# Weight parts made anew or kept in SBUF, a later turn in the attention, and the decode of the second layer's weights spread over three engines

## The chip, the cores and the metric

The kernel runs on one core of a Trainium2 chip. The metric is the device time of one execution in microseconds (us), the median of three timed runs. Engines are called by the names of the profile: PE (TensorE, the matmuls), PEld (its weight loads), DVE (VectorE), ACT (ScalarE), POOL (GpSimd) and SP (the queue that issues most DMAs).

## The reference, cut to what matters

```python
# attention: batch 4, heads 8, sequence 576, head size 64
q_s = softmax(q, axis=-1); k_s = softmax(k, axis=sequence)
kv  = einsum('bhsd,bhse->bhde', k_s, v)
x   = einsum('bhsd,bhde->bhse', q_s, kv)           # as 2304 tokens x 512
# first layer: 4 experts of width 1024, every token through all of them
out = sum_e p[:, e] * (relu(x @ w1[e]) @ w2[e])
# second layer, width 2048; its two weights come as 64-bit floats
h = out @ w_in; g = h * sigmoid(1.702 * h); result = g @ w_out
```

## The kernel before, in words

All matmuls are made of split numbers: an operand is cut into a high part and the rest (names ending in `h`/`l` or `_hi`/`_lo`), and a product is three matmuls, high by high, high by low and low by high. The high part is a cast on ACT, the low part a subtraction on POOL or DVE.

**Units.** A layer is cut into units of 256 hidden columns: 16 in the first layer (4 experts by 4), 8 in the second. The tokens are cut into groups 0 (1024 tokens), 1 (512) and 2 (768). Each layer makes two passes over its units, one for group 0 and one for groups 1 and 2 together. One visit of a unit is an *inst* (51 of them, numbers 0 to 50 are the suffixes in the names `a11_7`, `w20_6`), and inst and group make a *step*. The first three units are done before group 0 is whole, for its left half L (insts 0 to 2) and then its right half R (insts 3 to 5).

**Weight parts.** From a unit's weights, loaded as `ra` (first matrix) and `rc` (second), come the parts `a11, a12, a22, s1` to `s4` (or `a11, a12, a21, a22` for insts 0 to 5) in ten buffers of pool `w1p`, and `w20, w21` in four buffers of `w2p`. On the first visit they are made (`hi_w1`, `lo_w1`, `hi_w2`, `lo_w2`) and stored to DRAM (`store_part`: `k_a<-a`, `k_s<-s`, `k_w<-w`); on later visits they are loaded from there (`new_part`: `a<-k_a`, `w<-k_w`). `again` says which.

**Order.** The order of the work is written out by hand: up to step 5 the string `START` names every operation in turn; from step 6 on `step()` runs five stages (`STAGES`), each of them a few matmul products (`m1` to `m7`), evictions (`p1c`, `u2c`, `u3c` on ACT, `u2a`, `u3a`, `p1a` on DVE), the activation of the step before (`rc lc` and so on: `h_hi` on ACT, `h_lo` on DVE) and, in the stages `TILES` and `REST`, the second product `mm2` of the step before: per tile of 128 tokens six matmuls `po`, then `acc` on DVE (on ACT the first time). At the end of a stage `prepare` makes parts of the next inst, and `pump` advances a background generator: the attention of batches 2 and 3 (`attention`, one list of turns per head pair, a new pair every 8 stages), later the decode of the 64-bit weights (`decode`, 32 tiles of 128x512, 1.25 yields per stage). Each engine runs its instructions in the order written, so one that waits holds up everything behind it on its engine.

**The lines that matter:** L491 the product `pb` of the attention (needs `dg`, L487 on DVE); L506 the product `pk`; L110 a helper for copies; L646 the stores of attention output (`x_moe<-xo`); L656 to L659 `to_x2`, which transposes the first layer's output (`pt`), copies it (`xt`) and stores it (`x_ffn<-xt`, through two buffers `xo`); L803 to L824 the decode: masks of the upper word (`ds`, `dt`), and the lower word times the exponent plus the rest (`do`); L885 and L889 `h_lo`; L952 `po`; L964 and L973 `acc`.

```python
turns = ["km", "qm qs", "", "", "kg kgm", "qe", "", "ks ksv", "qu qn", "ke", "", "", "pk", "", "bd"]
"moe": ("-m5 -u3c m1 p1c -u3a", "m2 p1a REST", "-m6 -rc -rb -m7 -lc -u2a",
        "m3 u2c m4 -lb -rd ra -ld la", "TILES"),
```

Of the kernel before, what the change touches and what calls it, by code (L numbers as in the profile page):

```python
# [22 lines left out]
def tile_linear_attention_moe_gelu(  # L23
# [609 lines left out]
    def put_x(j, t0, w, src, eng, first):  # L633

        d, o = t0, None
        while d < t0 + w:
# [12 lines left out]
    def to_x2(i, ti, lt):
# [417 lines left out]
    def step(k_, tiles, before):  # L1067
# [65 lines left out]
        oa22:1 rz:1_2 rr:1_2 bd0:1_2 bd1:1_2@A qu:1_0 qs:1_1@G oa12:1 ha12:2 kg:1_1 qe:1_2 y0:s1 rz:1_0 kgm:1_1 rr:1_0
        q:1_3 ha22:2 bd0:1_0 qu:1_2 la12:2@G bd1:1_0@A qe:1_1 pk:1_3 ow20:0 la22:2@G z0:s1 qu:1_1 qp:1_2 qp:1_0 qr:1_2
        rc:6 qr:1_0 qn:1_2@G rz:1_3 qm:1_3 a1:s2 rr:1_3 bd0:1_3 c1:s2 bd1:1_3@A kdg:1_1 qp:1_1 oa12:0 qs:1_3@V t1:1_2
        qT1:1_2@A qr:1_1 ow21:0 qe:1_3 ks:1_1 a2:s2 ksv:1_1 qn:1_1@G ra:s2 px1:1_2 la:s2 ke:1_1 oa22:2 xf1:1_2@V
        t0:1_2 pk:1_1 qu:1_3 oa11:2 qT0:1_2@V ow20:1 wh0:2 t0:1_1 qp:1_3 qn:1_0@V px0:1_2 wh1:2 qT0:1_1@A qr:1_3
        wl1:2@G rz:1_1 xf0:1_2@A rr:1_1 c2:s2 bd1:1_1@V rc:s2 oa21:0 bd0:1_1 lc:s2 t1:1_0 qn:1_3@G t0:1_0 qT1:1_0@A
        px0:1_1 oa12:2 qT0:1_0@A px1:1_0 xf0:1_1@V px0:1_0 xf1:1_0@A wl0:2@V t0:1_3 xf0:1_0@V qT0:1_3@A ha11:3 t1:1_3
        t1:1_1 qT1:1_3@V px0:1_3 ha21:3 qT1:1_1@V px1:1_3 xf0:1_3@V ha12:3 px1:1_1 xf1:1_3@A y2:s1 xf1:1_1@V ow21:2  # L1140
        open Hb12:b0 y3:s1 z2:s1 Lb12:b0@V ha22:3 y0:s2 ow20:2 z3:s1 Hb22:b0 y1:s2 z0:s2 Lb22:b0@V wh0:3 wh1:3 ha11:4
        y2:s2 z1:s2 y3:s2 z2:s2 ha21:4 z3:s2 a1:s3 c1:s3 St1:b0@V Ht1:b0 ha12:4 ha22:4 a2:s3 Lt1:b0@G c2:s3 ra:s3
# [134 lines left out]
```

## Time and profile before

| | us |
|---|---|
| median of three timed runs (1230.03 to 1230.43) | 1230.19 |
| the profiled execution, its own time | 1235.11 |
| its span, first to last instruction | 1233.3 |
| PE busy | 1209.0 (98%) |
| DVE busy | 850.4 (69%) |
| ACT busy | 464.7 (38%) |
| POOL busy | 358.7 (29%) |

The chain of work that ended last lies on PE for 86% of the span and on DVE for 9%. The mean DMA rate is 183 GB/s. The granted TensorE clock is full in all but one of the 40 slices of the page. In the trace an entry in square brackets is the engine's idle time in front of an instruction and what ended it.

### The profile page before, as it was taken

What the parts mean: (1) busy time and instruction counts of PE and PEld (TensorE: products, weight loads), DVE (VectorE), ACT (ScalarE), POOL (GpSimd) and SP (SyncE); (2) the same over time, 40 slices, a digit from 0 to 9 for tenths busy, and PEclk for the clock granted to TensorE, in tenths of its full rate; (3) what the DMA queues carried; (4) which work ended last, traced back from release to release, by engine and by line L of the source; (5) the groups of instructions that cost most, each with busy time, mean ns of one, the idle gap of its engine ahead of it and who ended that gap; (6) DMA issues with size and microseconds to landing.
All of it is one profiled execution on the core that took longest, in us unless ns stands there. A gap on an engine that the chain in (4) does not pass through costs nothing.

```text
span 1233.3 us, 17497 instructions
## 1 busy us (share of the span) xinstructions
PE 1209.0 (98%) x6276; PEld 1043.9 (85%) x6276; DVE 850.4 (69%) x1416; ACT 464.7 (38%) x1010; POOL 358.7 (29%) x389
## 2 busy tenths in 40 slices
PE   8999899999999999999999999999999999999998
PEld 7878688887888899899899889898788889899997
DVE  7875778767567759998999975577355774454554
ACT  5544345433434352222122222145645544333332
POOL 4424657554553001111112331025454500000000
PEclk9999899999999999999999999999999999999999
DMA  8884966664566366666566632535655655334323
GB/s 199 250 303 141 324 210 203 204 230 149 198 217 226 105 198 213 212 209 211 194 194 221 202 110 69 196 121 186 232 203 213 228 170 161 111 107 122 108 92 86
DMA packets 134423, 225.86 MB, mean 183 GB/s; under 512 B 30400, under 2 KB 62144, under 8 KB 133696
## 3 DMA queue, kind: packets, MB, share of 16 engines
q1 hardware_dynamic: 124832, 220.02, 55.2%
q10 hardware_dynamic: 9504, 4.72, 1.3%
q8 instruction: 50, 0.82, 0.3%
q14 instruction: 37, 0.30, 0.1%
HBM read 137.40 MB, written 87.29 MB: 182 GB/s over the span
## 4 chain that ended last, share of the span: by engine, by line
PE 86%; DVE 9%; DMA 4%; ACT 1%; issue 1%; SPq 0%; POOL 0%; ACTq 0%; DVEq 0%
PE po L952 43%; PE px L836 21%; PE pz L836 10%; PE py L836 5%; DVE acc L964 2%; DVE h_lo L885 2%; DMA w64o<-in_moe_w_out 1%; PE pk L506 1%; PE p L378 1%; DMA x_ffn<-xt 1%; PE ca_R L836 1%; PE cc_R L836 1%; DMA q<-in_q 1%; DVE dso L803 1%; PE px L531 1%
## 5 line engine op out<-in xcount | busy, mean ns | idle before, releaser
L952 PE MATMUL po<-w,h_hi 128*128 128x512 f32 x1728 | 538.4, 393 | 2.4 <-DVE xt L110 2.0
L952 PEld LDWEIGHTS po<-w,h_hi 128*128 128x128 f32 x1728 | 320.8, 189 | 65.2 <-DVE xt L110 2.9
L952 PE MATMUL po<-w,h_lo 128*128 128x512 f32 x864 | 337.7, 391 | 3.2 <-DVE h_lo L885 3.2
L964 DVE SCALAR_TENSOR_TENSOR acc<-po,pr,acc 128x512 f32<-128x512 f32 x270 | 194.6, 745 | 70.1 <-PE po L952 69.7
L952 PEld LDWEIGHTS po<-w,h_lo 128*128 128x128 f32 x864 | 162.8, 188 | 39.4 <-DVE h_lo L885 4.5
L110 ACT COPY u<-px 128x384 f32<-128x384 f32 (+2 forms) x138 | 65.3, 473 | 237.7 <-PE px L836 230.3
L973 DVE TENSOR_TENSOR acc<-po,acc 128x512 f32<-128x512 f32 x126 | 85.7, 689 | 58.5 <-PE po L952 57.4
L866 DVE TENSOR_TENSOR u<-pz,u 128x384 f32<-128x384 f32 (+2 forms) x138 | 75.4, 546 | 52.9 <-ACT u L110 52.1
L774 POOL TENSOR_TENSOR s<-s,s 128x256 fp32r<-128x256 f32 x94 | 80.1, 860 | 74.2 <-ACT s L768 59.7
L787 POOL TENSOR_TENSOR w<-rc,w 128x512 fp32r<-128x512 f32 x46 | 60.4, 1314 | 86.6 <-ACT w L781 71.2
L774 POOL TENSOR_TENSOR a<-ra,a 128x256 fp32r<-128x256 f32 x69 | 53.4, 774 | 90.0 <-ACT a L768 80.0
L879 ACT ACTIVATE h_hi<-px 128x256 fp32r<-128x256 f32 (+2 forms) x45 | 21.8, 484 | 144.3 <-PE px L836 144.2
L885 DVE SCALAR_TENSOR_TENSOR h_lo<-u,h_hi 128x256 fp32r<-128x256 f32 (+2 forms) x90 | 63.7, 732 | 12.5 <-ACT h_hi L879 12.3
L823 POOL TENSOR_TENSOR doi<-doi,dti 128x512 f32<-128x512 f32 x16 | 21.0, 1312 | 161.1 <-DVE doi L820 155.0
L762 POOL TENSOR_TENSOR s<-ra 128x256 f32<-128x256 f32 x48 | 40.5, 844 | 75.8 <-DMA ra<-wi 49.8
L866 DVE TENSOR_TENSOR p<-py,p 128x384 f32<-128x384 f32 (+2 forms) x69 | 37.8, 548 | 33.6 <-PE py L836 30.1
L781 ACT CAST w<-rc 128x512 fp32r<-128x512 f32 x48 | 29.6, 620 | 72.2 <-PE po L952 71.5
L879 ACT ACTIVATE h_hi<-u 128x256 fp32r<-128x256 f32 (+2 forms) x90 | 46.3, 515 | 16.0 <-DVE u L866 16.0
L823 POOL TENSOR_TENSOR doo<-doo,dto 128x512 f32<-128x512 f32 x16 | 21.3, 1330 | 103.7 <-DVE doo L820 91.6
L110 ACT COPY p<-px 128x384 f32<-128x384 f32 (+2 forms) x69 | 32.9, 477 | 37.7 <-PE px L836 37.5
L768 ACT CAST s<-s 128x256 fp32r<-128x256 f32 x96 | 36.8, 404 | 24.0 <-POOL s L762 17.1
L889 DVE TENSOR_TENSOR h_lo<-sc,h_hi 128x512 fp32r<-128x512 f32 (+2 forms) x24 | 13.4, 559 | 44.3 <-ACT h_hi L881 44.3
(312 smaller groups left out, 2470.2 us busy)
## 6 DMA issues: line engine op xcount, KB each, us to landing
w<-k_w SPq DMA_DIRECT2D x54, 512.0 KB, 4.5
k_w<-w SPq DMA_DIRECT2D x48, 512.0 KB, 5.1
a<-k_a SPq DMA_DIRECT2D x84, 256.0 KB, 2.8
k_s<-s SPq DMA_DIRECT2D x84, 256.0 KB, 5.2
s<-k_s SPq DMA_DIRECT2D x84, 256.0 KB, 3.3
k_a<-a SPq DMA_DIRECT2D x75, 256.0 KB, 5.2
ra<-in_moe_w SPq DMA_DIRECT2D x19, 512.0 KB, 4.3
rc<-in_moe_w SPq DMA_DIRECT2D x16, 512.0 KB, 6.1
```

The source lines that it names most:

```text
L110: (eng.copy if eng is A else eng.tensor_copy)(o, i)
L762: G.tensor_tensor(out=o, in0=block_w(m, l), in1=block_w(m, r), op=op)
L774: eng.tensor_tensor(out=lo, in0=block_w(m, x), in1=hi.bitcast(F32), op=ALU.subtract)
L787: eng.tensor_tensor(out=lo, in0=raw[m, 1][:, c, :], in1=hi.bitcast(F32), op=ALU.subtract)
L823: G.tensor_tensor(out=o, in0=o, in1=t.bitcast(F32), op=ALU.add)
L836: T.matmul(ps, a[:, kk, :], b[:, kk, :], start=(start and n == 0), stop=(stop and n == 5), skip_group_check=True,)
L866: return lambda _: V.tensor_tensor(out=y[o], in0=y[ps], in1=y[o], op=ALU.add)
L879: A.activation(hi, y[c], AF.Relu)
L885: V.scalar_tensor_tensor(out=lo, in0=y[c], scalar=0.0, in1=hi.bitcast(F32), op0=ALU.max, op1=ALU.subtract)
L952: T.matmul(ps, a, b, start=(n == 0), stop=(n == 3 * FT - 1))
L964: V.scalar_tensor_tensor(out=acc[ti], in0=ps, scalar=pe, in1=acc[ti], op0=ALU.mult, op1=ALU.add)
L973: V.tensor_tensor(out=acc[ti], in0=ps, in1=acc[ti], op=ALU.add)
```

## The change

It has eight edits.

1. Insts 3 and 4 (the right half of units 1 and 2) use the parts of insts 1 and 2, which stay in SBUF (`HOME`); the right half visits the units in the order 1, 2, 0, so that only inst 5 loads parts back.
2. `w20` and `w21` are no longer stored and loaded back, but made anew at each visit (`again` is true for them in inst 5 alone). `rc` is loaded for each visit.
3. They are made at the end of stages 2 and 3 of an inst's first step, not 1 and 3.
4. In the attention of batches 2 and 3, `ks ksv` and all later turns come one stage later.
5. Its stores `x_moe<-xo` are issued by ACT, not by SP.
6. `xt` is always copied by ACT (before: by DVE in the second layer's steps), and the first `acc` of the second layer by DVE (before: ACT).
7. The decode of a tile takes 5 instructions on DVE (before 7), 2 on ACT (0) and 2 on POOL (1).
8. A filler of 432 instead of 56 words at the right end of SBUF.

```diff
-        turns = [... "kg kgm", "qe", "", "ks ksv", ...]
+        turns = [... "kg kgm", "qe", "", "", "ks ksv", ...]
-            copy(V if stage[1] else A, o, pt.rearrange("p k t -> p (k t)"))
+            copy(A, o, pt.rearrange("p k t -> p (k t)"))
-    turns = [(g, "L") for g in range(AHEAD)] + [(g, "R") for g in range(AHEAD)]
+    turns = [(g, "L") for g in range(AHEAD)] + [(g, "R") for g in (*range(1, AHEAD), 0)]
+    HOME = {AHEAD + n: 1 + n for n in range(AHEAD - 1)}
...
-        names = (PLAIN if m < NPLAIN else STRASSEN) + ("w20", "w21")
+        if m in HOME:
+            continue
+        names = PLAIN if m < NPLAIN else STRASSEN
         again.update({(m, x): (u, x) in had for x in names})
+        again.update({(m, x): m == NPLAIN - 1 for x in ("w20", "w21")})
...
+        V.tensor_scalar(
+            out=t, in0=top, scalar1=3, scalar2=0x007FFFF8, op0=ALU.logical_shift_left, op1=ALU.bitwise_and
+        )
         yield
-        V.tensor_scalar(
-            out=s, in0=s, scalar1=float(896 << 20), scalar2=8.0, op0=ALU.subtract, op1=ALU.mult
-        )
+        A.activation(o, low, AF.Copy, scale=2.0**-52)
+        A.activation(s, s, AF.Copy, bias=-float(896 << 23), scale=8.0)
+        yield
         V.scalar_tensor_tensor(
             out=s, in0=top, scalar=-(1 << 31), in1=s, op0=ALU.bitwise_and, op1=ALU.bitwise_or
         )
-        yield
-        V.tensor_scalar(
-            out=t, in0=top, scalar1=3, scalar2=0x007FFFF8, op0=ALU.logical_shift_left, op1=ALU.bitwise_and
-        )
         V.tensor_tensor(out=t, in0=t, in1=s, op=ALU.bitwise_or)
         yield
-        V.scalar_tensor_tensor(
-            out=o, in0=low, scalar=2.0**-52, in1=s.bitcast(F32), op0=ALU.mult, op1=ALU.mult
-        )
+        G.tensor_tensor(out=o, in0=o, in1=s.bitcast(F32), op=ALU.mult)
         G.tensor_tensor(out=o, in0=o, in1=t.bitcast(F32), op=ALU.add)
...
-                if s in (1, 3) and (m, s // 2) not in W2:
+                if s in (2, 3) and (m, s - 2) not in W2:
```

What this does to the order of the instructions, at three places. On PE, in step 7, after the product `pz4` and ahead of the four tiles `po3_0` to `po3_3` of step 6 (batch 2, head pair 0 of the attention). Before:

```order
L836 MATMUL pz4_0_1644<-t1lA_1191,s1_7_1489 128x512
L836 MATMUL pz4_0_1644<-t1hA_1190,s1_7_1489 128x512
L491 MATMUL pb_2_0_0_1670<-dg2_0_0_1633,ones_88 96x128
L952 MATMUL po3_0_1673<-w20_6_1439,h_hi_91 128x512 x2
L952 MATMUL po3_0_1673<-w20_6_1439,h_lo_92 128x512
```

With the change:

```order
L837 MATMUL pz4_0_1603<-t1lA_1167,s1_7_1452 128x512
L837 MATMUL pz4_0_1603<-t1hA_1166,s1_7_1452 128x512
L953 MATMUL po3_0_1628<-w20_6_1428,h_hi_91 128x512 x2
...
L953 MATMUL po3_3_1652<-w20_6_1428,h_lo_92 128x512
L953 MATMUL po3_3_1652<-w21_6_1458,h_hi_91 128x512 x2
L953 MATMUL po3_3_1652<-w21_6_1458,h_lo_92 128x512
L491 MATMUL pb_2_0_0_1683<-dg2_0_0_1592,ones_88 96x128
```

The product `pb`, which needs `dg` from DVE, stands behind the four tiles instead of ahead of them.

On DVE, in the decode, around tile o2 (`dso2`, `dto2`, `doo2`) and the `h_lo<-px` of inst 22 that the tiles wait for. Before:

```order
L803 TENSOR_SCALAR dso2_6212<-w64o2_6190 128x512
L804 TENSOR_SCALAR dso2_6212<-dso2_6212 128x512
L866 TENSOR_TENSOR p123_1_6209<-py23_1_6217,p123_1_6209 128x256
L964 SCALAR_TENSOR_TENSOR acc16_10_4620<-po22_10_6225,pr_89,acc16_10_4620 128x512
L964 SCALAR_TENSOR_TENSOR acc16_11_4629<-po22_11_6233,pr_89,acc16_11_4629 128x512
L808 TENSOR_SCALAR dso2_6212<-dso2_6212 128x512
L811 SCALAR_TENSOR_TENSOR dso2_6212<-w64o2_6190,dso2_6212 128x512
L815 TENSOR_SCALAR dto2_6213<-w64o2_6190 128x512
L818 TENSOR_TENSOR dto2_6213<-dto2_6213,dso2_6212 128x512
L885 SCALAR_TENSOR_TENSOR h_lo_92<-px22_2_6071,h_hi_91 128x384
```

With the change:

```order
L807 TENSOR_SCALAR dso2_6174<-w64o2_6150 128x512
L808 TENSOR_SCALAR dso2_6174<-dso2_6174 128x512
L811 TENSOR_SCALAR dto2_6175<-w64o2_6150 128x512
L867 TENSOR_TENSOR p123_1_6169<-py23_1_6180,p123_1_6169 128x256
L967 SCALAR_TENSOR_TENSOR acc16_10_4540<-po22_10_6188,pr_89,acc16_10_4540 128x512
L967 SCALAR_TENSOR_TENSOR acc16_11_4549<-po22_11_6196,pr_89,acc16_11_4549 128x512
L818 SCALAR_TENSOR_TENSOR dso2_6174<-w64o2_6150,dso2_6174 128x512
L821 TENSOR_TENSOR dto2_6175<-dto2_6175,dso2_6174 128x512
L886 SCALAR_TENSOR_TENSOR h_lo_92<-px22_2_6030,h_hi_91 128x384
```

The subtraction and multiplication on `dso2` has gone from DVE, and ahead of this `h_lo` two instructions of the tile stand where four stood. The two new copies on ACT stand between `p123_1` and `h_hi<-px22_2`.

On SP, in the second layer, inst 36 (`rc37` is the load for inst 37). Before:

```order
L745 DMA rc37_8740<-wo32_106 128x2x512
L713 DMA k_w21_35_8663<-w21_35_8660 128x1024
L713 DMA k_s3_36_8691<-s3_36_8688 128x512
L713 DMA k_a22_36_8695<-a22_36_8692 128x512
L713 DMA k_s4_36_8699<-s4_36_8696 128x512
L713 DMA k_a11_37_8737<-a11_37_8734 128x512
L713 DMA k_w20_36_8785<-w20_36_8782 128x1024
L713 DMA k_a12_37_8818<-a12_37_8815 128x512
```

With the change:

```order
L749 DMA rc37_8745<-wo32_106 128x2x512
L717 DMA k_s3_36_8697<-s3_36_8694 128x512
L717 DMA k_a22_36_8701<-a22_36_8698 128x512
L717 DMA k_s4_36_8705<-s4_36_8702 128x512
L717 DMA k_a11_37_8742<-a11_37_8739 128x512
L717 DMA k_a12_37_8818<-a12_37_8815 128x512
```

Two stores of 512 KB are gone from each visit in a first pass.

## Rows read from the trace of the kernel before

**Rows 1.** Line 1 of the page: busy time, share of the span, instructions.

```profile
PE 1209.0 (98%) x6276; PEld 1043.9 (85%) x6276; DVE 850.4 (69%) x1416; ACT 464.7 (38%) x1010; POOL 358.7 (29%) x389
```

**Rows 2.** Stretches: from:to, length, busy us (count) per engine, clock, DMA share, GB/s.

```profile
446.00:715.00 269.00, 264.65 (x1463) 238.69 (x1462) 249.32 (x457) 64.70 (x155) 49.87 (x41) 1.00 0.63 204
...
100.00:150.00 50.00, 45.32 (x186) 36.15 (x185) 33.67 (x42) 20.87 (x45) 32.52 (x36) 0.93 0.81 251
250.00:300.00 50.00, 48.31 (x231) 39.28 (x230) 36.49 (x54) 19.54 (x42) 25.32 (x29) 0.97 0.59 207
```

**Rows 3.** Timeline of PE, 126 to 140 us: start, us, instruction, idle before.

```profile
136.29 0.74 PE L491 MATMUL pb<-dg,ones 128*96 128x128 f32 x2 [4.68 <-DVE dg L487]
136.68 1.20 PE L952 MATMUL po<-w,h_hi 128*128 128x512 f32 x2
...
139.38 1.05 PE L952 MATMUL po<-w,h_hi 128*128 128x512 f32 x2
```

**Rows 4.** Timelines of DVE, ACT and SP ahead of that wait.

```profile
132.81 0.69 DVE L885 SCALAR_TENSOR_TENSOR h_lo<-px,h_hi 128x512 fp32r<-128x512 f32 x1 [2.26 <-ACT h_hi L879]
134.30 1.93 DVE L487 TENSOR_SCALAR dg<-ident,gm 128x128 f32<-128x128 f32 x1
...
131.36 0.40 ACT L768 CAST a<-ra 128x256 fp32r<-128x256 f32 x1 [5.28 <-issue]
...
123.16 0.72 SPq L713 DMA_DIRECT2D k_w<-w  x1
...
124.77 1.00 SPq L741 DMA_DIRECT2D ra<-in_moe_w  x1
```

**Rows 5.** Timelines of DVE, POOL and PE, 283 to 300 us.

```profile
285.81 7.04 DVE L885 SCALAR_TENSOR_TENSOR h_lo<-u,h_hi 128x512 fp32r<-128x512 f32 x1 [0.27 <-ACT h_hi L879]
...
285.07 1.79 POOL L466 TENSOR_TENSOR qn<-q,qu 96x768 f32<-96x768 f32 x1 [0.55 <-DVE qu L462]
...
294.17 1.61 PE L506 MATMUL pk<-v,ke 96*128 96x129 f32 x12 [1.69 <-DVE acc L964]
```

**Rows 6.** Timeline of PE in the decode: the three waits, and a tile's start.

```profile
606.21 0.51 PE L952 MATMUL po<-w,h_lo 128*128 128x512 f32 x1 [1.55 <-DVE h_lo L885]
606.55 0.63 PE L952 MATMUL po<-w,h_hi 128*128 128x512 f32 x2
...
607.92 0.62 PE L952 MATMUL po<-w,h_hi 128*128 128x512 f32 x2
...
708.05 0.44 PE L836 MATMUL pz<-b22hmoe,s 128*128 128x384 f32 x1 [1.19 <-DVE u L866]
...
713.58 0.50 PE L952 MATMUL po<-w,h_lo 128*128 128x512 f32 x1 [1.60 <-DVE h_lo L885]
```

**Rows 7.** Timeline of DVE, 596 to 612 us: the `h_lo` of inst 22.

```profile
605.60 0.55 DVE L885 SCALAR_TENSOR_TENSOR h_lo<-px,h_hi 128x384 fp32r<-128x384 f32 x1
```

**Rows 8.** Groups by line and shape: count, busy us, mean ns, idle before.

```profile
L964 DVE SCALAR_TENSOR_TENSOR acc<-po,pr,acc 128x512 f32<-128x512 f32 x270 | 194.6, 745 | 70.1 <-PE po L952 69.7
L787 POOL TENSOR_TENSOR w<-rc,w 128x512 fp32r<-128x512 f32 x46 | 60.4, 1314 | 86.6 <-ACT w L781 71.2 <-PE po L952 15.3
L781 ACT CAST w<-rc 128x512 fp32r<-128x512 f32 x48 | 29.6, 620 | 72.2 <-PE po L952 71.5 <-DMA rc<-in_moe_w 0.7
L823 POOL TENSOR_TENSOR doo<-doo,dto 128x512 f32<-128x512 f32 x16 | 21.3, 1330 | 103.7 <-DVE doo L820 91.6 <-issue 7.2 <-PE px L836 4.9
L820 DVE SCALAR_TENSOR_TENSOR doo<-w64o,dso 128x512 f32<-128x512 uint32 x16 | 10.9, 682 | 0.0
L808 DVE TENSOR_SCALAR dso<-dso 128x512 int32<-128x512 int32 x16 | 7.6, 477 | 0.1
```

**Rows 9.** Timelines of PE and DVE, 862 to 882 us; then landings of `x_ffn<-xt`.

```profile
873.70 0.72 PE L952 MATMUL po<-w,h_hi 128*128 128x512 f32 x2 [1.97 <-DVE xt L110]
...
869.33 0.69 DVE L110 COPY xt<-pt 128x512 f32<-128x512 f32 x1 [3.72 <-DMA x_ffn<-xt]
...
DMA to landing us min/median/max: 2.6/3.9/8.6
```

More of the change, by code (lines that the diff above doesn't have):

```diff
@@ L542, in attend2 @@
             group(g)
-        turns = ["km", "qm qs", "", "", "kg kgm", "qe", "", "ks ksv", "qu qn", "ke", "", "", "pk", "", "bd"]
+        turns = ["km", "qm qs", "", "", "kg kgm", "qe", "", "", "ks ksv", "qu qn", "ke", "", "", "pk", "", "bd"]
         turns += [f"t{g} qT{g}" for g in range(NG_)] + [""] + [f"px{g} xf{g}" for g in range(NG_)]
@@ L631, in forms, with put_x @@
         then()
-    def put_x(j, t0, w, src, eng, first):
+    def put_x(j, t0, w, src, eng, first, by=S_):
         d, o = t0, None
@@ L645, in put_x @@
                     copy(eng or A, o[:, d - t0 : w], src[:, d - t0 : w])
-                S_.dma_start(out=x_d["moe", i][:, j, d - g0 : d - g0 + m], in_=o[:, d - t0 : d - t0 + m])
+                by.dma_start(out=x_d["moe", i][:, j, d - g0 : d - g0 + m], in_=o[:, d - t0 : d - t0 + m])
             d += m
@@ L723, in put_away @@
             stores.pop(0)[1]()
-    stage = [0, False]
+    stage = [0]
     def put_old():
@@ L825, in decode @@
         yield
-    acc = {}
+    acc, begun = {}, set()
     x2 = []
@@ L898, in go @@
                     b = f"b{kh + 1}{1 + (i == 'R')}"
-                    mm(y["c" + x], W1[m, f"a{ft + 1}{kh + 1}"], X[0, b], kh == 0, kh == 1)
+                    mm(y["c" + x], W1[HOME.get(m, m), f"a{ft + 1}{kh + 1}"], X[0, b], kh == 0, kh == 1)
                 return go
@@ L936, in mm2 @@
     def mm2(g, i, lt, m, ho):
-        kind, e, f, pas, first, last = units[g]
+        kind, e, f, pas, _, last = units[g]
         t0, n = SPANS[i]
@@ L949, in product @@
                 hh, hl = h_hi[:, ft, s], h_lo[:, ft, s]
-                wh, wl = W2[m, ft]
+                wh, wl = W2[HOME.get(m, m), ft]
                 for a, b in ((hh, wh), (hh, wl), (hl, wh)):
@@ L956, in total @@
             ps = y["ps"]
+            first = (kind, ti) not in begun
+            begun.add((kind, ti))
             if first:
@@ L970, in total @@
             if first:
-                A.copy(acc[ti], ps)
+                V.tensor_copy(acc[ti], ps)
             else:
@@ L1133, in tile_linear_attention_moe_gelu @@
[L1133 to L1142, printed above, removed]
@@ L1147, in tile_linear_attention_moe_gelu @@
+        ha12:6 hs2:6 la12:6@V y3:s4 z2:s4 hs3:6 ls2:6@V z3:s4 ls3:6@V hs1:6 ls1:6@G St4:b0@G
     """
     open_pool("edge", bufs=1, side="right")
-    pools["edge", "p"].tile([P, 56], F32, name="edge")
+    pools["edge", "p"].tile([P, 432], F32, name="edge")
     open_pool("xp0", bufs=2, side="right")
@@ L1185, in tile_linear_attention_moe_gelu @@
             new["l" + x] = lambda e, m=m, x=x: lo_w1(m, x, e or G)
-            new["o" + x] = lambda _, m=m, x=x: first_stores.pop((m, x))()
+            new["o" + x] = lambda _, m=m, x=x: first_stores.pop((m, x), lambda: None)()
         for c in range(FT):
@@ L1189, in tile_linear_attention_moe_gelu @@
             new[f"wl{c}"] = lambda e, m=m, c=c: lo_w2(m, c, e or G)
-            new[f"ow2{c}"] = lambda _, m=m, c=c: first_stores.pop((m, f"w2{c}"))()
+            new[f"ow2{c}"] = lambda _, m=m, c=c: first_stores.pop((m, f"w2{c}"), lambda: None)()
         add(m, new)
```

31 lines of the change are left out of this document (19 added, 12 removed).

## The prediction

> **What bounds the kernel now.** I read the page first, then the stretches, then the timelines around each gap on PE. PE is busy for 1209.0 of 1233.3 us of span [rows 1], so the change can give back only what lies in the few stalls of PE, and the time that PE loses at the lower clock behind them; work that goes from DVE, SP or ACT is worth nothing by itself. The stretches [rows 2] show two places after the start with a granted clock below 1.00, 100 to 150 us (0.93) and 250 to 300 us (0.97), and a long stretch from 446 to 715 us (the decode) in which DVE is busy for 249.32 of 269 us while PE loses little. The timelines then give four places, called A to D. What is printed in brackets behind a PE row is the idle time that the change could remove.
>
> A, a wait of 4.68 us at 136.29 for `dg` [rows 3]. PE had nothing to do after the last `pz`, since `pb` stands ahead of the `po` tiles. Behind it the first `po` tile takes 139.38 - 136.68 = 2.70 us, where a tile at full clock takes 607.92 - 606.55 = 1.37 us [rows 3, 6]: the clock had dropped to the lower level, 1.2 GHz, after the idle time. I take two tiles of it, 2 x 1.33 = 2.7 us; the clock of 0.93 over 50 us would be 3.5 [rows 2]. So A is worth 7.4 us, 8.2 at most. The chain ahead of it [rows 4]: `ra` issued at 124.77 behind a `k_w` store, ACT's cast of it at 131.36 after 5.28 us of idle time, `h_lo` at 132.81, `dg` at 134.30, which took 1.93 us.
>
> B, a wait of 1.69 us at 294.17 [rows 5]. An `h_lo` from SBUF took 7.04 us on DVE, ten times the 0.69 us of the like instruction in [rows 4], while POOL was at work from 285.07 on. With 0.03 x 50 = 1.5 us for the clock [rows 2] this is worth 3.2 us.
>
> C, three waits for DVE in the decode, 1.55 + 1.19 + 1.60 = 4.34 us [rows 6]. DVE is late there because of its own queue: `h_lo` of inst 22 starts at 605.60 [rows 7] though PE wanted it 1.55 us before 606.21.
>
> D, 1.97 us at 873.70 [rows 9]. `po` waits for a bank that `xt` has to empty, and `xt` waited 3.72 us for the DMA `x_ffn<-xt` that holds its buffer; landings of this DMA run from 2.6 to 8.6 us with a median of 3.9, and this was a late one.
>
> **The change part by part.** *Later turns (edit 4), fewer stores and loads (edit 2).* `pb` goes behind the four tiles of step 6, 4 x 1.37 = 5.5 us of PE work that needs no `dg`. PE would reach `pb` about 5.5 us later than 131.6, that is at 137.1, and `dg` ended at 136.23. What PE needs first instead is `h_lo`, for the third matmul of the first tile; it ended at 132.81 + 0.69 = 133.50, and PE wants it about 132.8, after the tiles' high parts. That would leave a wait of 0.7 us; but `ra`, issued just behind a `k_w` store [rows 4], loses that store, whose 0.72 us of issue and 512 KB of traffic stood ahead of it, so I take the wait as gone too. A: -7.4 us (bounds -3.7, if half of it comes back, and -8.2).
>
> *Parts made anew (edit 2, 3).* 48 more casts on ACT at 0.620 us (29.8 us) and 48 more subtractions on POOL at 1.314 us (63 us) [rows 8]. ACT is at 38% and POOL at 29% [rows 1], and each is made a step ahead of use, beside PE's work, so I cost them at nothing; without that cover a late part costs PE its 1.3 us per visit. The 46 stores and 52 loads of 512 KB that go make room in DMA. `rc` is loaded 24 times more, which is less traffic than the loads that go. SP loses 104 issues; ACT gains 20 (`x_moe`, edit 5), of about half a microsecond each by SP's 0.72 to 1.00 us [rows 4], beside 62% idle time: nothing.
>
> *HOME (edit 1), filler (edit 8).* No stall of PE beyond A lies in 100 to 150 us, so dropped casts and stores there gain nothing; for the filler no row shows a price, and I take 0.
>
> *Longer POOL work and B.* The profiled execution took 1235.11 us, 4.92 above the median 1230.19, so part of its stalls is its own. Whether B is in the usual execution can't be seen; the instruction order around it changes (POOL's runs shift by a stage), and I count half: -1.6 us (bounds 0 and -3.2).
>
> *Decode (edit 7).* DVE loses, per tile, one `dso` (0.477) and one `doo` (0.682) [rows 8], 1.16 us, for 32 tiles 37 us (the input tiles' `dsi` taken as the same). ACT gains two copies for each; their price is not in the trace, the nearest row is the cast of the same shape at 0.620, so 64 x 0.62 = 40 us beside ACT's 64.70 of 269 [rows 2]. POOL gains one multiplication, about 1.33 by the addition of the same shape [rows 8], 43 us, and some 22 parts of edit 2 at 1.314, 29 us: 50 becomes 122 us of 269. An instruction of DVE that meets one on POOL waits for it; that gives back part of the 37 us. I take DVE at about 225 us (84%) for 249. Of the three waits two are shorter than the 1.16 us plus what the backlog of the tile before gives up as well, so I take -3.7 of -4.34 us (bounds 0 and -4.34; a loss is the first rival).
>
> *Copies (edit 6).* `xt` on ACT no longer queues behind DVE's `acc`; the first `acc` moves to DVE at about the 0.69 of its additions. Neither sets an end. D depends on the landing: two `k_w` stores of 512 KB fall out of the traffic ahead of it, so I take its 8.6 us as about 6, and D: -1.9 us (bounds 0 and -2.2).
>
> *New waits.* The moved work on ACT and POOL will open some wait that I can't name: +1.5 us, which is about one of C's three (bounds 0 and +4).
>
> **Sum**, against the profiled execution: -7.4 - 1.6 - 3.7 - 1.9 + 1.5 = -13.1, so 1235.11 - 13.1 = 1222.0; less the 4.92 us by which it stood above the median, 1217.1, rounded to 1217.0. The best ends, -8.2 - 3.2 - 4.3 - 2.2, give 1212.3; that the new order also shortens something at the start, 2 us, gives 1210.
>
> **The rivals.** *GpSimd holds VectorE in the decode (slower).* The mechanism is B's: as POOL runs without a gap, an SBUF instruction on DVE waits for the whole run. With the change a multiplication and an addition of POOL stand back to back, 2 x 1.33 = 2.66 us per tile. If each holds DVE for all of it, DVE falls back by 2.66 - 1.16 = 1.5 us per tile, where it now has a 7% margin. Then `h_lo` is late in every step: 32 tiles x 4 yields / 1.25 per stage / 5 stages = 20.5 steps, at the mean 1.45 us of C's waits 29.7 us, of which 4.3 are there now: +25.4. With A, B and D as forecast (-10.9), 1230.2 - 10.9 + 25.4 = 1244.7. It decides as soon as the hold per tile is over 1.16 us; half of the steps late is about no gain. For it speaks B [rows 5]; against it that `h_lo` on 7 us is a run of nine POOL instructions, and that half of DVE's work (`acc`, 745 ns in 270 cases [rows 8]) reads PSUM and keeps its time. Chance 0.09. The Trainium skill, "GPSIMD Engine Reference", section "8. Key points", says that GpSimd shares its SBUF interfaces with VectorE and contends with VectorE instructions that run in a two-port mode or take two SBUF inputs. The trace agrees as far as it goes: 7.04 us for the `h_lo` with two SBUF inputs.
>
> *The waits move instead of going.* `h_lo` is late behind `ra` (0.7 us at A), and C and D stay since the join on DVE now waits for ACT's copies and the same late landing holds `xt` on ACT. Then -6.7 - 1.6 + 1.5 = -6.8: 1223.4. For it: three engines in a row per tile in place of one. Against it: each link has a stage, 269 us by 102 stages or 2.6 us, for about 1.2 us of work. Chance 0.17.
>
> *Nothing gained.* The later turn puts `pb` or `ks` of another head pair where A was, with the same idle time and the same clock; C comes back as POOL's work doubles. Then only D and the new waits remain, -0.4: 1229.8. For it: the eight stages of a pair meet five stages of a step, so each pair meets other places. Against it: of these pairs only one stalls now. Chance 0.08.
>
> **How the numbers follow.** Forecast 0.66, waits that move 0.17, nothing 0.08, slower 0.09. A measurement of this kernel can tell about 0.2%, 2.5 us, from no change: faster is below 1227.7 (0.66 + 0.17 = 0.83), the same up to 1232.7 (0.08), slower above (0.09). The range goes from 1210 to 1227: it holds the forecast with its bounds and the second rival, and leaves out the two others (0.17).
>
> **What would show it.** Right: no wait for `dg` and a clock of 1.00 in 100 to 150 us; no wait over 1 us for `h_lo` or `u` in the decode, with DVE at about 225 of 269 us and POOL at about 120; landings of `x_ffn<-xt` at most 6.5 us and no stall at `po` near 870 us; POOL busy for some 460 us in all, ACT for some 530. Wrong: `h_lo` rows of 2 us and more behind POOL's pairs and a PE stall in most decode steps (first rival); stalls for `h_lo` in the first layer ended by `ra` or by ACT (second); a new wait for `dg`, `ks` or `ksv` with a clock below 0.95 (third).

## The result, and the profile after

The changed kernel takes 1241.32 us (four runs, 1239.77 to 1243.76), where the kernel before took 1230.11 beside it: ratio 1.0094, 95% interval 1.0076 to 1.0112. It is 11 us slower, where 13 us faster were forecast, and outside the range. The profiled execution took 1240.66 us.

The page's first line, as [rows 1]:

```profile
PE 1209.9 (98%) x6276; PEld 1047.2 (85%) x6276; DVE 879.5 (71%) x1360; ACT 517.7 (42%) x1114; POOL 491.4 (40%) x469
```

PE's work is the same. DVE has 56 instructions fewer than before and is busy for 29 us *more*: its instructions got longer. The stretches, as [rows 2], with two added:

```profile
446.00:715.00 269.00, 267.17 (x1474) 240.18 (x1474) 242.56 (x385) 110.92 (x239) 131.86 (x90) 1.00 0.58 185
150.00:200.00 50.00, 43.76 (x208) 35.69 (x208) 37.44 (x52) 18.75 (x41) 27.49 (x30) 0.95 0.56 170
200.00:250.00 50.00, 47.00 (x213) 38.59 (x212) 35.61 (x53) 19.49 (x42) 22.32 (x25) 0.91 0.39 117
100.00:150.00 50.00, 45.73 (x195) 36.97 (x194) 35.95 (x44) 20.90 (x43) 34.62 (x39) 0.97 0.76 229
250.00:300.00 50.00, 48.76 (x240) 40.11 (x239) 36.44 (x60) 21.06 (x47) 28.70 (x32) 1.00 0.47 146
```

From 150 to 250 us PE is idle for 9.2 us and runs at a clock of 0.95 and 0.91. Before, PE was busy for the whole of these 100 us at 1.00:

```profile
150.00:200.00 50.00, 50.00 (x249) 41.21 (x248) 37.35 (x62) 21.57 (x46) 30.84 (x35) 1.00 0.67 213
200.00:250.00 50.00, 50.00 (x243) 41.10 (x242) 37.16 (x61) 22.27 (x48) 30.89 (x36) 1.00 0.73 222
```

This is the attention of batches 2 and 3, whose turns edit 4 moves. PE's waits from 125 to 325 us (waited for: us, times, longest) sum to 14.4 us, before to 6.4 (4.7 for `dg` [rows 3] and 1.7 for `acc` [rows 5]):

```profile
PE px L531 <- DVE acc L967: 7.5, 3, 5.0
PE pb L491 <- DVE acc L967: 3.9, 1, 3.9
PE po L953 <- DVE gm L485: 3.0, 1, 3.0
```

The wait for `dg` [rows 3] is gone, but at the same place `pb` now waits for `acc`, which stands behind a long `h_lo` (timelines of PE and DVE):

```profile
139.25 0.46 PE L491 MATMUL pb<-dg,ones 128*96 128x128 f32 x2 [3.90 <-DVE acc L967]
...
134.73 3.81 DVE L886 SCALAR_TENSOR_TENSOR h_lo<-p,h_hi 128x512 fp32r<-128x512 f32 x1
```

The four other waits are new. The longest of them, in the timelines of PE, DVE and POOL:

```profile
194.99 0.85 PE L531 MATMUL px<-qT,kvbd 128*128 128x288 f32 x1 [4.99 <-DVE acc L967]
...
184.83 0.89 DVE L448 TENSOR_REDUCE qm<-q 96x12 f32<-96x768 f32 x1
185.65 7.50 DVE L886 SCALAR_TENSOR_TENSOR h_lo<-u,h_hi 128x512 fp32r<-128x512 f32 x2
193.07 1.20 DVE L886 SCALAR_TENSOR_TENSOR h_lo<-p,h_hi 128x512 fp32r<-128x512 f32 x1
194.20 2.71 DVE L967 SCALAR_TENSOR_TENSOR acc<-po,pr,acc 128x512 f32<-128x512 f32 x4
...
185.00 1.72 POOL L466 TENSOR_TENSOR qn<-q,qu 96x768 f32<-96x768 f32 x1 [1.56 <-DVE qu L462]
186.68 1.47 POOL L451 TENSOR_TENSOR q<-q,qm 96x768 f32<-96x768 f32 x1
188.12 1.43 POOL L778 TENSOR_TENSOR s<-s,s 128x256 fp32r<-128x256 f32 x2
189.51 0.72 POOL L766 TENSOR_TENSOR s<-ra,s 128x256 f32<-128x256 f32 x1
190.20 1.26 POOL L791 TENSOR_TENSOR w<-rc,w 128x512 fp32r<-128x512 f32 x1
```

Two `h_lo` together take 7.50 us instead of 2 x 0.69 while POOL works without a gap from 185.00 to 194.86; `acc`, which must empty the banks that PE's next products go to, starts only behind them. It is the hold of [rows 5] at a new place. POOL's `qn` and the next head pair's `q` stand back to back: a new pair starts every 8 stages, and `qu qn`, moved from turn 8 to 9, meets `qm qs` of the next pair, turn 1. In the same way `ks ksv`, moved from 7 to 8, meets `km`, turn 0.

### The profile page after: what moved, and what is told of

Same layout as the page of the kernel before. It is cut to its first block, busy times and chain, and to the rows that moved or that the text cites. A ratio compares the mean times of both kernels' runs of the same rounds, so it can differ in the third digit from the quotient of the medians.

```text
span 1238.9 us, 17554 instructions
## 1 busy us (share of the span) xinstructions
PE 1209.9 (98%) x6276; PEld 1047.2 (85%) x6276; DVE 879.5 (71%) x1360; ACT 517.7 (42%) x1114; POOL 491.4 (40%) x469
## 4 chain that ended last, share of the span: by engine, by line
PE 81%; DVE 13%; DMA 2%; issue 2%; ACT 1%; POOL 1%; SPq 1%; POOLq 0%; ACTq 0%; DVEq 0%
PE po L953 40%; PE px L837 19%; PE pz L837 9%; PE py L837 5%; DVE h_lo L886 4%; DVE acc L967 2%; DMA w64i<-in_moe_w_in 1%; PE pk L506 1%; PE p L378 1%; DVE u L867 1%; PE cc_L L837 1%; PE ca_L L837 1%; PE cc_R L837 1%; PE ca_R L837 1%; PE px L358 1%
## 5 line engine op out<-in xcount | busy, mean ns | idle before, releaser
L791 POOL TENSOR_TENSOR w<-rc,w 128x512 fp32r<-128x512 f32 x94 | 134.8, 1435 | 318.6 <-ACT w L785 317.6
L886 DVE SCALAR_TENSOR_TENSOR h_lo<-u,h_hi 128x256 fp32r<-128x256 f32 (+2 forms) x90 | 93.7, 1066 | 10.8 <-ACT h_hi L880 10.5
L785 ACT CAST w<-rc 128x512 fp32r<-128x512 f32 x96 | 58.8, 615 | 1.0 <-DMA rc<-in_moe_w 1.0
L823 POOL TENSOR_TENSOR doi<-doi,dsi 128x512 f32<-128x512 f32 x16 | 28.1, 1754 | 54.2 <-DVE dsi L818 39.3
L876 ACT ACTIVATE sc<-px 128x256 f32<-128x256 f32 (+2 forms) x25 | 12.2, 487 | 84.7 <-PE px L837 83.5
L886 DVE SCALAR_TENSOR_TENSOR h_lo<-px,h_hi 128x256 fp32r<-128x256 f32 (+2 forms) x45 | 24.5, 544 | 31.7 <-ACT h_hi L880 31.6
```

The lines of the kernel that those rows point to most:

```text
L785: A.copy(W2[m, c][0], raw[m, 1][:, c, :])
L791: eng.tensor_tensor(out=lo, in0=raw[m, 1][:, c, :], in1=hi.bitcast(F32), op=ALU.subtract)
L886: V.scalar_tensor_tensor(out=lo, in0=y[c], scalar=0.0, in1=hi.bitcast(F32), op0=ALU.max, op1=ALU.subtract)
```

## The experiments

All were timed beside the kernel before, which took 1229.2 to 1231.5 us in these timings, and each ratio is to the timing beside it. The last two columns are the sums of PE's waits in the profile of each run, 125 to 325 us (attention) and 446 to 730 us (decode).

| run | us | ratio, interval | attention | decode |
|---|---|---|---|---|
| before | 1230.1 | 1 | 6.4 | 4.4 |
| the change | 1241.3 | 1.0094 (1.0076 to 1.0112) | 14.4 | 4.2 |
| e1 | 1231.2 | 1.0003 (0.9989 to 1.0017) | 8.7 | 3.9 |
| e2 | 1238.1 | 1.0065 (1.0044 to 1.0086) | 15.3 | 2.5 |
| e3 | 1231.2 | 0.9998 (0.9985 to 1.0011) | 9.3 | 2.4 |
| e4 | 1247.6 | 1.0134 (1.0108 to 1.0160) | 13.4 | 8.9 |
| e5 | 1235.8 | 1.0028 (1.0017 to 1.0038) | 10.2 | 4.5 |
| e6 | 1234.8 | 1.0035 (1.0020 to 1.0049) | 11.2 | 4.3 |
| e7 | 1243.7 | 1.0096 (1.0081 to 1.0111) | 15.0 | 4.2 |
| e8 | 1227.2 | 0.9957 (0.9942 to 0.9972) | 5.4 | 0.9 |
| e9 | 1230.3 | 0.9999 (0.9988 to 1.0011) | 11.0 | 0.8 |
| e10 | 1236.9 | 1.0059 (1.0043 to 1.0076) | 4.6 | 10.5 |
| e11 | 1231.2 | 1.0012 (1.0002 to 1.0022) | 13.5 | 0.8 |
| e12 | 1236.7 | 1.0059 (1.0044 to 1.0074) | 12.7 | 4.2 |
| e13 | 1223.4 | 0.9935 (0.9920 to 0.9950) | 6.4 | 0.8 |
| e14 | 1241.9 | 1.0092 (1.0065 to 1.0119) | 14.6 | 4.3 |
| e15 | 1227.7 | 0.9967 (0.9953 to 0.9982) | 7.3 | 1.2 |
| e16 | 1228.7 | 0.9984 (0.9973 to 0.9994) | 7.7 | 0.9 |
| e17 | 1229.7 | 1.0005 (0.9993 to 1.0017) | 6.6 | 4.2 |
| e18 | 1221.0 | 0.9928 (0.9910 to 0.9946) | 4.6 | 1.7 |

### Which edit costs

**e1**, the change with edit 4 undone:

```diff
-"qe", "", "", "ks ksv",
+"qe", "", "ks ksv",
```

> The changed kernel with edit 4 alone undone: ks ksv and the later turns of the attention stand where they stood before. Theory T (the turns): with the later turn, qu qn of one head pair and qm qs of the next fall into the same stage (and ks ksv with km), so that GpSimd gets two instructions of 1.47 us back to back with the weight parts behind them, and VectorE about 4.7 us of attention work ahead of acc; the waits of PE at 139, 165, 195, 223 and 280 us come from that. Then this run loses the waits at 165, 195, 223 and 280 and their clock (some 14 us), gets back the wait for dg at 136 (7 us), and takes 1228 to 1234 us. Theory S (the stage of w20 and w21, edit 3): the lower part made at the end of stage 2 stands in the middle of the run of parts; then this run stays at 1239 to 1244. Theory W (GpSimd is fuller everywhere, by the parts made anew and the decode): 1239 to 1244 too.

1231.2: theory T has the time right. One empty turn costs 10 us in the change (by the ratios 11). Of the waits 8.7 us are left, 3.0 of them a new one for `k`.

**e2**, the change with edit 3 undone:

```diff
-if s in (2, 3) and (m, s - 2) not in W2:
+if s in (1, 3) and (m, s // 2) not in W2:
```

> The changed kernel with edit 3 alone undone: w20 and w21 are made at the ends of stages 1 and 3 again. Theory T (the turns): the two attention instructions on GpSimd still stand together, 1238 to 1244 us, with waits of 3 us and more left between 130 and 300 us. Theory S (the stage): the runs on GpSimd fall apart, no wait over 2 us between 150 and 300, 1227 to 1233. Theory W: 1239 to 1244.

1238.1, with waits of 5.0 us still there: theory S falls as the main cause; some 3 us may belong to it, its interval touches that of the change.

**e3**, both undone.

> The changed kernel with edits 3 and 4 undone. Theory T: as with edit 4 undone, within 3 us of that run. Theory S: as with edit 3 undone, within 3 us of that run. If both matter: 1223 to 1229, below both of them. Theory W (the parts made anew and the decode fill GpSimd everywhere): 1238 to 1244 still.

As e1: if edit 3 costs anything, it does so only beside edit 4.

**e4**, the change with edit 7 undone: the old body of `decode`.

> The changed kernel with edit 7 alone undone: the decode as before, with seven instructions on VectorE and one on GpSimd. Theories T and S: the decode is worth little either way, 1239 to 1244, with the waits between 130 and 300 us unchanged and 3 to 7 us of waits between 446 and 730. Theory W: GpSimd is relieved by 42 us there, the waits near 688, 700 and 722 us (4.3 us) go, and this run takes 1235 to 1238.

1247.6: no theory said this. The decode edit is worth 5 us in the change by the ratios (6 by the times), and theory W is wrong on it; yet PE's waits in the decode are then twice those of before (8.9 for 4.4), with the same decode. Something else in the change costs there.

**e7**, the kernel before with edit 4 alone.

> The kernel before with edit 4 alone (the later turns). Theory TP: the meeting of qn and q costs here too; minus the wait for dg at 136 us (7.4 us with its clock) plus the waits of 5.2, 3.2, 1.4 and 1.4 us and their clock (some 14 to 16): 1235 to 1241 us. Rival, that edit 4 costs only with edit 3 or with the dropped stores, which let GpSimd run without gaps: 1222 to 1228.

1243.7, by 3 us above the end that theory TP gave: edit 4 alone makes up the whole loss, in the old surroundings too. Its waits from 125 to 325 us are of the change's three kinds, the one for `gm` longer (5.0 for 3.0) and the one of `pb` shorter (2.3 for 3.9):

```profile
PE px L531 <- DVE acc L964: 7.7, 3, 5.0
PE po L952 <- DVE gm L485: 5.0, 1, 5.0
PE pb L491 <- DVE acc L964: 2.3, 1, 2.3
```

### What in the later turns costs

**e5** moves only `ks ksv` (VectorE's `k` meets `mx`), **e6** only `qu qn` (GpSimd's `qn` meets `q`), both in the change:

```diff
+e5: "qe", "", "", "ks ksv qu qn", "ke", "", "", "pk", "", "bd"
+e6: "qe", "", "ks ksv", "", "qu qn ke", "", "", "pk", "", "bd"
```

> The changed kernel, but of the later turns only ks ksv stays a stage later (in one stage with qu qn, and with km of the next head pair); qu qn and all behind stand as before the change. GpSimd's qn and the next pair's q no longer fall into one stage; VectorE still gets k, mx and qu in a row. Theory TP (the pair of 1.47 us instructions on GpSimd starts the long holds of h_lo): the waits at 195 and 223 us go, those at 165 and 280 (1.4 us each) stay, 1229 to 1234 us. Theory TV (VectorE's own pile of about 4.7 us ahead of acc): stays at 1238 to 1243.

> The changed kernel, but of the later turns only qu qn stays a stage later (in the stage of qm qs of the next head pair, with ke behind it); ks ksv and all from pk on stand as before the change. GpSimd's two instructions stay together, VectorE's pile of k and mx is gone. Theory TP: waits of 3 to 5 us near 195 and 223 us with a clock below 0.95, 1237 to 1243 us. Theory TV: 1229 to 1234.

1235.8 and 1234.8; by the ratios 3 and 4 us above e1, which shares all other edits. Neither theory has it alone: each meeting costs, and the whole edit, with the turns from `pk` on, which no run moved alone, some 10 us.

**e12**, the change with `qs` a stage later, away from `qn`:

```diff
-"km", "qm qs", "", "",
+"km", "qm", "qs", "",
```

> The changed kernel with one difference: qs (the instruction of 1.47 us on q) goes a stage later than qm, so that it no longer stands behind qn of the head pair before in the same stage; all the later turns stay. Theory TP (the two together start the long holds of h_lo): the waits at 195 and 223 us fall below 2 us each, 1231 to 1236 us. Theory TV and others (VectorE's pile, or the later px and xf): 1239 to 1244.

1236.7: some 4 us less than the change. The waits of `px` (three, 5.0 the longest) are at most 1.2 us now, but the one for `pb` grew to 6.1: an `h_lo` at 132.95 is now held for 7.06 us, through a run of weight parts (POOL's `q` had ended at 131.0).

**e14**, the change with `q` and `qn` on VectorE:

```diff
-"km", "qm qs", ... "qu qn"
+"km", "qm qs@V", ... "qu qn@V"
```

> The whole change, with the attention's two 1.47 us instructions (q, qn) of batches 2 and 3 on VectorE (about 0.95 us each there, by k at the same size) in place of GpSimd. Theory TP (GpSimd's runs that begin with them hold h_lo): the long holds at 185 and 218 us go and with them 8 us or more: 1229 to 1234 us. Theory P (any run of GpSimd without a gap holds h_lo, the weight parts alone too): holds of 3 us and more stay, 1236 to 1243. Theory TV (VectorE's own pile): slower, 1241 to 1247.

1241.9, no better. The holds are gone: no `h_lo` from 120 to 310 us takes over 2 us. But the timeline of DVE ahead of a wait of 4.0 us shows what came instead:

```profile
156.54 0.95 DVE L494 TENSOR_TENSOR k<-k,pb 96x768 f32<-96x768 f32 x1
157.41 1.56 DVE L474 TENSOR_REDUCE mx<-k 96x128 f32<-96x768 f32 x1
158.88 0.93 DVE L460 TENSOR_REDUCE qu<-q 96x12 f32<-96x768 f32 x1
159.85 0.69 DVE L461 TENSOR_SCALAR qu<-qu 96x12 f32<-96x12 f32 x1
160.58 0.23 DVE L462 RECIPROCAL qu<-qu 96x12 f32<-96x12 f32 x1
160.84 1.17 DVE L466 TENSOR_TENSOR qn<-q,qu 96x768 f32<-96x768 f32 x1
161.94 0.94 DVE L448 TENSOR_REDUCE qm<-q 96x12 f32<-96x768 f32 x1
162.91 0.95 DVE L451 TENSOR_TENSOR q<-q,qm 96x768 f32<-96x768 f32 x1
163.78 2.71 DVE L967 SCALAR_TENSOR_TENSOR acc<-po,pr,acc 128x512 f32<-128x512 f32 x4
```

Attention work of 7.2 us (156.54 to 163.78) stands ahead of `acc`. With the later turns two head pairs fall into one stage, and on either engine, in the change and in e14, their work makes DVE late at `acc`.

### What eats the decode's gain

**e8**, the kernel before with edit 7 alone, **e10**, before with the parts made anew alone:

```diff
+e10: again ... (u, x) in had and (m < NPLAIN or x[0] != "w")
```

> The kernel before with edit 7 alone (the decode in four stages). The run with edit 7 undone was 6 us slower than the whole change, so the edit helps at least beside the parts made anew. Theory DW (these parts on GpSimd, edit 2, cost in the decode what edit 7 gives back): here, without them, the waits in the decode go from 4.3 us to under 1, and the time is 1225 to 1228 us. Theory DH (GpSimd's back-to-back multiplication and addition hold VectorE): waits of 4 us or more stay in the decode, 1229 to 1234.

> The kernel before with the core of edit 2 alone, from inst 6 on: w20 and w21 are made anew at each visit, at the ends of stages 1 and 3, with no stores and loads; the decode is the old one. Theory DW: the waits in the decode grow from 5.7 to about 14 us, VectorE there to about 259 of 269 us, 1237 to 1242 us. Rival: the made parts lie beside other work, 1229 to 1233.

Both by theory DW, e10 at the near end: 1236.9 us and 10.5 us of waits, where 1237 to 1242 and about 14 were expected (the 5.7 us before is 4.4 in the table). The decode stretch of e8, e10 and e4, one line each (PE, PEld, DVE, ACT, POOL, clock, DMA share, GB/s):

```profile
446.00:715.00 269.00, 268.09 (x1483) 242.92 (x1482) 232.84 (x400) 101.02 (x220) 111.57 (x78) 1.00 0.62 203
```

```profile
446.00:715.00 269.00, 260.08 (x1424) 231.57 (x1423) 261.10 (x442) 71.33 (x165) 76.76 (x59) 1.00 0.56 176
```

```profile
446.00:715.00 269.00, 262.83 (x1436) 235.29 (x1435) 258.93 (x439) 74.28 (x173) 77.31 (x59) 0.99 0.57 178
```

With edit 7 DVE falls from 249.3 [rows 2] to 232.8 us and the waits to 0.9. With the parts made anew POOL has 27 us more, and DVE, with no work added, rises to 261.1 of 269: PE then waits for `h_lo` nine times:

```profile
PE po L952 <- DVE h_lo L885: 7.4, 9, 1.8
PE pz L836 <- DVE u L866: 1.9, 2, 1.2
```

**e9**, e3 with edit 2 undone too (parts stored and loaded back):

```diff
-names = PLAIN if m < NPLAIN else STRASSEN
+names = (PLAIN if m < NPLAIN else STRASSEN) + ("w20", "w21")
```

> The run with edits 3 and 4 undone, with edit 2 undone as well: w20 and w21 are stored on the first visit and loaded back on later ones, so GpSimd and ScalarE do not make them anew. HOME, the ACT stores, the copies and the decode in four stages stay. Theory DW (the parts made anew fill GpSimd in the decode, hold VectorE and cost what the decode edit gives): 1222 to 1227 us against some 1231 of that run, VectorE at about 233 of 269 us and waits below 1.5 us in all in the decode. Rival (what cancels the decode's gain is elsewhere, in HOME or the copies): 1229 to 1233.

DVE at 229.9 us and waits of 0.8 in the decode, as theory DW has it, but the time is 1230.3, as the rival has it: the waits of the attention are 11.0, with a hold of 6.59 us at 209 us that e8 does not have.

**e13**, e9 with edit 5 undone (stores of the attention by SP), **e17**, the whole change with edits 4 and 5 undone:

```diff
-put_x(j, ..., y["px", g], A, None, A)
+put_x(j, ..., y["px", g], A, None)
```

> The run with edits 2, 3 and 4 undone, with edit 5 undone too (the attention's stores go by SP again). That run has a hold of 6.59 us of an h_lo at 209 us and a wait of 3.5 us behind it which the kernel before with the decode edit alone does not have. Theory X (issues that SP no longer makes bring ra earlier and with it GpSimd's run of parts onto this h_lo): the hold at 209 us goes or moves, 1225 to 1229 us. Rival (it comes from HOME or the copies): 1229 to 1232 with the hold in place.

> The whole change with edits 4 and 5 undone (turns as before, the attention's stores by SP); the weight parts made anew (2, 3), HOME, the copies and the decode in four stages stay. If those two edits are what makes the change slow and edit 2 takes some 3 us in the decode from what edit 7 gives: 1225 to 1228 us, with 5 to 7 us of waits in the decode. If edit 5 costs only in the one surrounding where it was undone (without edits 2 to 4): 1229 to 1233, as with edit 4 alone undone.

e13 takes 1223.4, 7 us (by the ratios 8) less than e9. But theory X has the wrong mechanism. The timelines of e9, DVE and then ACT:

```profile
208.53 0.77 DVE L885 SCALAR_TENSOR_TENSOR h_lo<-u,h_hi 128x512 fp32r<-128x512 f32 x1 [0.37 <-ACT h_hi L879]
209.22 6.59 DVE L885 SCALAR_TENSOR_TENSOR h_lo<-p,h_hi 128x512 fp32r<-128x512 f32 x1
...
206.52 0.81 ACTq L646 DMA_DIRECT2D x_moe<-xo  x2
207.38 0.59 ACT L110 COPY u<-px 128x512 f32<-128x512 f32 x1 [0.88 <-PE px L836]
```

and of e13:

```profile
208.62 2.29 DVE L885 SCALAR_TENSOR_TENSOR h_lo<-u,h_hi 128x512 fp32r<-128x512 f32 x2
210.83 0.68 DVE L885 SCALAR_TENSOR_TENSOR h_lo<-p,h_hi 128x512 fp32r<-128x512 f32 x1
...
208.55 0.59 ACT L110 COPY u<-px 128x512 f32<-128x512 f32 x1 [0.99 <-PE px L836]
```

POOL's run stands at the same distance in both: `a<-ra` starts 3.69 us after `qn` (203.86 to 207.55, and 205.32 to 209.01). What differs is ACT: in e9 it issues three stores ahead of `u`, which starts 3.52 us after `qn` instead of 3.23. DVE waits 0.37 us for `h_hi`, and the next `h_lo` is held for the whole run. PE is not what differs: its last matmul of the `px` that `u` copies starts 2.80 us after `qn` in both. Two more profiles fit: e3, with the same stores, has the same hold of 6.59 us (`u` 3.51 us after `qn`), and e8, without them, has none (3.29). In e17 edit 5's undoing changes nothing against e1 (1.0005 and 1.0003): what it costs depends on where the hold falls, here a matter of 0.3 us. e17 and e13 differ by edits 2 and 3 alone: 6.2 us, 0.7% by the ratios, with decode waits of 4.2 and 0.8. With edit 5 in place edit 2 makes no difference to the time (0.9998 in e3, 0.9999 in e9): the 1.6 us of decode waits that e9 saves stand against 1.7 us more in the attention.

### Other tries

**e11**, e9 with `kg kgm` a turn earlier; **e15** and **e16**, e8 with `qn`, or `qn` and `q`, on VectorE (`@V`).

> As the run with edits 2, 3 and 4 undone, and kg kgm of the attention a stage earlier, so that dg is on hand long before the product pb: the wait at about 135 us is answered by making dg earlier, not by taking pb later. If that wait is bound to dg alone: 5 to 7 us less than without this, 1217 to 1222. If h_lo behind the late ra, or the GpSimd run that follows, takes its place: 0 to 2 us less. If gm and dg now fall into another GpSimd run: no gain, waits for gm or dg at another place.

> The kernel before with edit 7 alone (1227.2 us) and qn on VectorE. Theory TP: the hold of 7 us at 285 us and the wait of 1.85 us behind it with its clock go: 1223 to 1226 us. Theory P: the parts alone hold it, 1226 to 1230.

> As that, with q on VectorE too. The wait for dg at 135 us stands behind q (in a GpSimd run that began with it), so by theory TP part of it goes as well: 1219 to 1224 us. Theory P: the parts alone, 1224 to 1230.

e11 is nearest to the last case of its expectation, no gain: `pm` and `po` wait for 2.4 and 7.2 us at other places, for `mx` and `k`, 1231.2. e15 and e16 are no better than e8 (1227.2), in the times of theory P. The hold at 285 us is gone in both, as theory TP has it, and in e16 the wait for `dg` is down to 2.4 us; but two waits of `px` for `acc` come, together 2.4 us in e15 and 4.5 in e16, as in e14.

**e18**, e13 with `dg` made by ScalarE:

```diff
-V.tensor_scalar_mul(y["dg"], ident, y["gm"])
+A.mul(y["dg"], ident, y["gm"])
```

> The best version so far (edits 1, 6, 7 and 8 alone, 1223.4 us), with dg (128x128, 1.94 us on VectorE at 133 us because GpSimd holds it) made by ScalarE. Theory P, that the hold alone makes this wait long: dg is ready about 1.3 to 1.5 us earlier, the wait of 4.4 us at 135 us shrinks to 3 and its clock loss stays: 1221 to 1223 us. If the hold only moves on to the next h_lo: 1223 to 1225. If ScalarE has no room ahead of h_hi there: 1225 to 1230.

1221.0, the best of all, though its interval overlaps that of e13. The timelines of PE, ACT and DVE:

```profile
133.51 0.74 PE L491 MATMUL pb<-dg,ones 128*96 128x128 f32 x2 [2.46 <-ACT dg L487]
...
133.06 0.40 ACT L487 ACTIVATE dg<-ident,gm 128x128 f32<-128x128 f32 x1 [0.71 <-DVE gm L485]
...
132.94 3.69 DVE L885 SCALAR_TENSOR_TENSOR h_lo<-u,h_hi 128x512 fp32r<-128x512 f32 x2
```

The wait falls from 4.4 to 2.5 us; the hold goes on to `h_lo`, which PE needs later.

## Why the prediction was wrong

**A, later turns: the step that failed.** "pb goes behind the four tiles" was right, and the wait for `dg` went. But at A's own place 3.9 of the 4.7 us came back as the wait for `acc`, and the term of -7.4 us (bounds -3.7 and -8.2) took for free that all later turns move with it. What the moved turns meet, eight stages on, was not looked at: e7 measures edit 4 alone at +0.96%, 12 us. The bound had no positive end, and the +1.5 us for new waits (at most +4) was far too small: from 125 to 325 us they sum to 14.4. A slip without effect: the 0.7 us for `h_lo` at A takes the 1.20 us of a pair of matmuls at the lower clock [rows 3]; with 0.63 [rows 6] it is 1.3. No such wait came.

**Parts made anew, costed at nothing.** "Made a step ahead of use, beside PE's work" was true of PE and not of DVE: no part is late, but POOL's work holds DVE where DVE has 7% of margin. Edits 2 and 3 cost 6.2 us or 0.7% (e17 against e13), edit 2 alone in the kernel before 0.59%, 7.3 us (e10), but nothing between e3 and e9, which both have the hold that comes with edit 5. Edit 5, also costed at nothing, costs 7 us in e9 and nothing in e1 against e17. The holds had been counted for the decode's own pair of instructions, with 225 us for DVE (242.56 measured) and 122 for POOL (131.86).

**Decode, -3.7 us: right by itself.** e8 takes 3.5 us of waits out of the decode and 0.43%, 5.3 us, off the time. In the change it only pays for edit 2. Edits 1, 6 and 8, taken at nothing but for D, show no worth of their own: 0.9935 with edit 7 (e13) and 0.9957 for edit 7 alone (e8), with intervals that overlap.

**B.** The hold of [rows 5] stands in e8, e10, e13 and e18 too (a wait of 1.7 us), so it belongs to the usual execution, and the whole of it could have been counted. In the change it is gone, as hoped, but others stand elsewhere.

**D, -1.9 us: counted twice, at least in part.** The largest landing is 6.5 us after the change, near the 6 forecast. But with the stores and the old copy in place it changes from profile to profile: 8.6 in [rows 9], 8.3 in e16, 6.7 to 7.0 in e7, e8 and e15, and the wait for `xt` near 870 us is 2.0, 1.1 and at most 0.4. So the wait is not in every execution, and what belonged to the profiled one alone was already in the 4.92 us taken off for it. How much D is worth in the usual execution no run shows.

**The rivals.** The first had the mechanism (GpSimd holds VectorE) and a time near the measured one (1244.7), at the wrong place, for the decode's pair: that the time is near is luck. Two of its figures are off: the 7 us of [rows 5] are a run of eight POOL instructions, not nine, and `acc` is a quarter of DVE's work in the decode (65.7 of 249.3 us), not half. The third had the place (another head pair, a clock below 0.95) but took the loss as equal to the gain. The runs chain up: edits 1, 6, 7, 8 together 0.9935 (e13), with 2 and 3 1.0005 (e17), with 5 1.0003 (e1), with 4 1.0094.

## What to carry to other kernels

When a step of a software pipeline is moved, list what it meets on every engine, with the period of the pipeline: here a turn moved by one stage meets the next item's turn eight stages earlier, on two engines at once. Work put on GpSimd is not free for VectorE: where VectorE was busy for 249.3 of 269 us, 27 us more on POOL made it busy for 12 us more (e10), so count POOL's added time partly as VectorE's. A stall found in one profiled execution is taken off once, either as a term or with the distance to the median; profiles of other kernels with the same code there tell whether it is one execution's.

## What the runs showed of the hardware

How long VectorE is held is not set by one GpSimd instruction. The `h_lo` of 0.69 us took 1.2 us beside some runs, 2 to 4 beside others, and 7.0 in [rows 5] and in e13, at the same run of POOL. In one stretch, 0.3 us of ACT's time went with the difference between 0.68 us (e13) and 6.59 us (e9). What decides is open. A small `dg` (128x128, one tensor read) was held too: 1.94 us in e13 (0.29 at 197.11 in the change), while ACT made it in 0.40 in e18.

It seems that POOL can be held as well. Where DVE came through, in e13, POOL's `s<-ra` took 2.39 us while DVE did its last two `h_lo`, `gm` and `dg` (second line: the same instruction in e9).

```profile
209.72 2.39 POOL L765 TENSOR_TENSOR s<-ra 128x256 f32<-128x256 f32 x1
...
208.71 1.18 POOL L765 TENSOR_TENSOR s<-ra 128x256 f32<-128x256 f32 x1
```

Elsewhere in e13 the same instruction takes 0.74 us.

The groups of the change show whom it hits; the mean of this `h_lo` was 1023 ns before:

```profile
L886 DVE SCALAR_TENSOR_TENSOR h_lo<-u,h_hi 128x512 fp32r<-128x512 f32 x26 | 34.5, 1351 | 6.0 <-ACT h_hi L880 5.9
L823 POOL TENSOR_TENSOR doi<-doi,dsi 128x512 f32<-128x512 f32 x16 | 28.1, 1754 | 54.2 <-DVE dsi L818 39.3 <-issue 14.8
L824 POOL TENSOR_TENSOR doi<-doi,dti 128x512 f32<-128x512 f32 x16 | 21.4, 1337 | 1.3
```

The multiplication on POOL takes 1754 ns, the addition of the same shape behind it 1337. That DVE holds it is not shown; no run took the multiplication alone. `acc`, which reads PSUM, keeps its time (744 ns, before 745 [rows 8]). The Trainium skill, "GPSIMD Engine Reference", section "8. Key points", names the shared SBUF interfaces and the kinds of VectorE instruction that contend; the trace agrees, 7.0 for 0.69 us. That a hold can last through eight GpSimd instructions in a row is told by the traces alone.
